# Retention and a gated MLP on one core: loads of two tokens to a partition, 64x64 quarters for every chunk, block 1 as Strassen

## The chip, the cores and the metric

The kernel runs on one core of a Trainium2 chip. A core has TensorE (matmuls into PSUM), VectorE, ScalarE, GpSimd and SyncE, each with its own queue of instructions that it works through in order; sixteen DMA engines serve the transfers that SyncE, ScalarE and GpSimd issue. The metric is the device time of one execution in microseconds. 304.59 us is the median of three runs of the kernel before (304.25 to 305.26).

## The reference

Eight batches of eight heads, 576 tokens and 64 columns go through a retention without softmax, and the 4608 resulting rows of 512 columns through an MLP with a cosine gate:

```python
scores = scale * np.matmul(q, k.transpose(0, 1, 3, 2))      # scale 1/8
Dmat = np.where(rel >= 0, gamma[:, None, None] ** rel[None, :, :], 0.0)
ret = scores * Dmat[None, :, :, :]
attn = np.matmul(ret, v)                                    # (8, 8, 576, 64)
x = attn.transpose(0, 2, 1, 3).reshape(4608, 512)
h = x @ w_in                                                # 512 x 2048
out = (h * np.cos(h)) @ w_out                               # 2048 x 512
```

All tensors are float32; the kernel multiplies in bf16.

## The kernel before

**Attention by chunks.** A batch is cut into four chunks of 128 tokens and one of 64 (`NCH` = 5). The decay is put into q and v: q is multiplied by gamma^position/8, v by gamma^-position (`decay`), k is only cast (`kcast`). For a chunk there are scores (k by q, both with the head's columns on partitions), a mask (`rt`, VectorE), the product with v, and a state: k transposed times v, summed over the chunks in the PSUM bank `st`, whose copy (`sb` in batches 0 and 1, `sn` later) gives the past's share to the next chunk. The result goes into `xt`, the MLP's input with columns on partitions (two ScalarE copies a chunk, split where the ring of `XR` = 1536 tokens wraps).

**Two ways to compute it.** Batches 2 to 7 use `quarters`: matmuls of 64x64, four of which use the four quarters of the array at once; `weave` interleaves two lists, one for each half of the rows, and a few products wait for an earlier one into the same bank. One call, a "visit", does past, own product and state of chunk r and the scores of chunk r+1 (of the next batch's chunk 0 after the last). Their k and q are turned by a DMA transpose (`turn_dma`). Batches 0 and 1 use `scores`, `rest`, `state_mm` and `state_copy`, with 128 tokens as the contraction. Their k and q come as quads (`quad`: four neighbouring tokens to a partition, two heads, all 512 tokens at once, runs of 1 KB), are cast by `quad_cast`, turned on TensorE against an identity (`quad_turn`: four matmuls and a copy), and k is turned back (`back`) for the state. Their last chunks are loaded as the later batches are: one token to a partition, runs of 256 B.

**MLP by blocks of 512 tokens.** Block j first computes h tile by tile (`mlp1`, 16 tiles `dt` of 128 columns: four matmuls of 512 tokens, a cosine on ScalarE into `cb`, a product on VectorE into `gt`), then the output. Blocks 0 and 1 do that plainly (`plain2`: four stripes of 128 tokens, each in four pieces of four matmuls, `out2` copies and stores). Blocks 2 to 8 use Strassen's seven products (`mlp2`) of half the size; sums of parts of `gt` (`ssum` into `ss`) and of w_out (`tsum` into `ts`, 16 of them, once) run on VectorE. The visits of batch j+1 stand between the products of block j; the casts and the DMA transposes of batch j+1 (`prep`) between the tiles of `mlp1`.

**The order.** Everything is written out by hand in `emit`; `Sched` adds the semaphores. Before the first tile of block 0 stand batch 0's quads, casts and turns, its chunks 0 to 2 and dummy matmuls (`idle`) that fill waits. Chunk 3 stands between the first tiles of block 0, which are cut into 256-token halves. Block 0's second product is 16 pieces, with batch 0's chunk 4, batch 1's turns, and its chunks 0 and 1 between them; block 1's first product is cut at 320 tokens, with batch 1's chunks 2 to 4; its second product, plain, has batch 2's five visits and the twelve remaining sums of w_out.

**Queues.** SyncE issues the loads in the order of `push`. GpSimd issues the weight loads, which cast to bf16: w_in slice 0 (`wi0`) once v of chunk 0 has landed, then the other three between casts, then four of w_out. A gate (`after`, "wi1") makes SyncE wait, ahead of the load of batch 0's chunk 4 and all of batch 1, until w_in slice 1 has landed. `pump` issues a load when its buffer among the 16 of `ld` is free in program order. ScalarE issues the stores.

The lines that the profile names: L264 loads, L287 and L293 weight loads, L299 copies and casts, L326 decay, L361/L409/L411 matmul groups, L433 and L704 masks, L502 and L504 cosine and gate, L526 and L544 Strassen sums, L660 `weave`.

Of the kernel before, what the change touches and what calls it, by code (L numbers as in the profile page):

```python
# [22 lines left out]
NR = 9  # L23
NL = 16
# [105 lines left out]
class _Kernel:  # L130
    def __init__(self, nc, es, q, k, v, w_in, w_out, out):
# [17 lines left out]
        self.QS = [sb(f"qs{i}", [128, 512], BF16) for i in range(4)]  # L149
        self.bQS = bufs(4)  # L150
        self.n_qs = 0
# [21 lines left out]
        self.SB = [sb(f"sb{i}", [128, NP * 128], BF16) for i in range(2)]  # L173
        self.bSB = [Buf() for _ in range(2)]
# [12 lines left out]
        self.IP = sb("ip", [128, NCH], F32)  # L187
        self.WV = sb("wv", [128, NCH * H_], F32)
        self.UQ = sb("uq", [128, NCH * H_], F32)
        self.IP4 = sb("ip4", [128, 4], F32)  # L190
        self.UQ4 = sb("uq4", [128, 4 * H_], F32)
        self.LG = sb("lg", [128, H_], F32)
        self.LP = sb("lp", [128, NCH * H_], F32)
        self.LP4 = sb("lp4", [128, 4 * H_], F32)
        self.bIP4, self.bUQ4, self.bLG, self.bLP, self.bLP4 = bufs(5)
        self.MK = sb("mk", [128, CH], BF16)
# [26 lines left out]
    def consts(self):  # L223
        s = self.s
        s.op("dve", lambda e: e.memset(self.IDLE.ap(), 0.0), writes=[self.bIDLE])
        s.op("pool", lambda e: e.iota(self.IP4.ap(), [[1, 4]], base=0, channel_multiplier=4,
                                      allow_small_or_imprecise_dtypes=True), writes=[self.bIP4])
        s.op("pool", lambda e: e.iota(self.IP.ap(), [[CH, NCH]], base=0, channel_multiplier=1,
                                      allow_small_or_imprecise_dtypes=True), writes=[self.bIP])
        s.op("dve", lambda e: e.memset(self.C_LN8.ap(), float(math.log(1.0 / 8.0))), writes=[Buf()])  # L230
        s.op("dve", lambda e: e.memset(self.C_PIH.ap(), float(math.pi / 2.0)), writes=[self.bC])
        for h in range(H_):
            t = s.op("dve", lambda e: e.memset(bass.AP(self.LG, h, [[H_, 128], [1, 1]]), self.lng[h]),
                     writes=[Buf()])
        self.bLG.w = [t]
        for t, b, fill, first, cmp in ((self.ID, self.bID, 1.0, 0.0, ALU.not_equal),
                                       (self.MK, self.bMK, 0.0, 1.0, ALU.is_ge)):
            s.op("dve", lambda e: e.memset(t.ap(), first), writes=[b])
            s.op("pool", lambda e: e.affine_select(t.ap(), t.ap(), pattern=[[1, CH]],
                                                   compare_op=cmp, fill=fill, base=0,  # L240
                                                   channel_multiplier=-1), reads=[b], writes=[b])
        for i in range(2):
            s.op("dve", lambda e: e.memset(self.SB[i].ap(), 0.0), writes=[self.bSB[i]])
        for lp, blp, ip, bip, n in ((self.LP4, self.bLP4, self.IP4, self.bIP4, 4),
                                    (self.LP, self.bLP, self.IP, self.bIP, NCH)):
            s.op("dve", lambda e: e.tensor_tensor(
                bass.AP(lp, 0, [[n * H_, 128], [H_, n], [1, H_]]), bass.AP(ip, 0, [[n, 128], [1, n], [0, H_]]),
                bass.AP(self.LG, 0, [[H_, 128], [0, n], [1, H_]]), ALU.mult), reads=[bip, self.bLG], writes=[blp])
        for t, b, sign, lp, blp in ((self.UQ4, self.bUQ4, 1.0, self.LP4, self.bLP4),
                                    (self.WV, self.bWV, -1.0, self.LP, self.bLP),  # L250
                                    (self.UQ, self.bUQ, 1.0, self.LP, self.bLP)):
            s.op("act", lambda e: e.activation(
                t.ap(), lp.ap(), AF.Exp, scale=sign, **(dict(bias=self.C_LN8.ap()) if sign > 0 else {})),
                reads=[blp, self.bC], writes=[b])
        s.op("act", lambda e: e.activation(self.JUNK.ap(), self.C_PIH.ap(), AF.Sin), reads=[self.bC])
# [3 lines left out]
    def fetch(self, key, src, dims, n):  # L259
        i = self.n_ld % NL  # L260
        self.n_ld += 1
        t = self.LD[i]
        dst = bass.AP(t, 0, [[DM, n]] + dims)
        t = self.s.dma("sp", f"ld{i}", lambda e: e.dma_start(dst, src), writes=[self.bLD[i]])  # L264
        self.got[key], self.busy[i] = i, True
        self.wtok[key] = t
# [5 lines left out]

    def load(self, b, r, xs="kqv"):
        ck = ck_of(r)
        for x in xs:
            src = bass.AP(self.src[x], (b * H_ * S_ + CH * r) * D_, [[D_, ck], [S_ * D_, H_], [1, D_]])
            self.fetch((x, b, r), src, [[D_, H_], [1, D_]], ck)

# [89 lines left out]
    def quad_turn(self, x, b, c, i, eng, bank=None):  # L368
# [10 lines left out]
        for u in (self.bKT if x == "k" else self.bQT)[s0:s0 + 4]:  # L379
            u.w.append(t)  # L380
# [669 lines left out]
```

## Time and profile before

| What | us |
|---|---|
| median of three runs | 304.59 (304.25 to 305.26) |
| the profiled execution | 302.51 |
| its span, first to last instruction | 300.6 |
| TensorE busy | 291.7 |
| VectorE busy | 222.7 |
| ScalarE busy | 169.8 |
| GpSimd busy | 107.0 |
| granted TensorE clock, mean | 0.999 |

A row of the table of stretches has the stretch (us from the span's start), its length, then for PE (matmuls), PEld (weight loads), DVE (VectorE), ACT (ScalarE) and POOL (GpSimd) the busy time and in brackets the instructions, then the granted clock, the share of the DMA engines (over 1 where packets overlap) and GB/s. A row of the chain, and of the timeline, has start, length, engine and what is done, written "out<-in"; in square brackets stands the idle time ahead of it and what ended it. A row of the groups has line, engine, operation, tiles, shapes and count, then busy time and mean ns of one, then the idle time ahead of the group. SPq and ACTq are the queues in which SyncE and ScalarE issue transfers.

### The profile page before, as it was taken

The numbers are of one execution on the slowest core, as the hardware profiler recorded it, in microseconds if no ns is written. First come the engines' busy times: TensorE is split into PE (matmuls) and PEld (weight loads), VectorE is DVE, ScalarE is ACT, GpSimd is POOL, SyncE is SP. The second block draws the span as 40 slices with busy tenths as digits, with TensorE's granted clock in tenths as the row PEclk, the third lists the DMA queues.
The fourth block names the chain that finished last, engine by engine and source line by source line (L and its number), as shares of the span: only waits on it lengthen the run. The fifth ranks groups of instructions, "written<-read, shape, count | busy, mean of one in ns | idle before, by whom it ended". The sixth has DMA issues, their size and how long they took to land.

```text
span 300.6 us, 7939 instructions
## 1 busy us (share of the span) xinstructions
PE 291.7 (97%) x3339; PEld 182.0 (61%) x3366; DVE 222.7 (74%) x422; ACT 169.8 (56%) x327; POOL 107.0 (36%) x127
## 2 busy tenths in 40 slices
PE   8899999999999999999999999999999999999995
PEld 3474455645454488548854776468646864684484
DVE  3666666767569997699669984998499749837963
ACT  6788535886247735673558355744575458416810
POOL 3670337656454653376445555454000000000000
PEclk9999999999999999999999999999999999999999
DMA  7999999999999998999999999999300130012013
GB/s 225 228 203 199 213 313 204 309 204 182 243 229 199 193 206 185 242 199 209 183 228 237 211 191 265 224 184 162 106 2 0 40 105 2 0 60 82 2 35 106
DMA packets 142419, 49.67 MB, mean 165 GB/s; under 512 B 126000, under 2 KB 141360, under 8 KB 142384
## 3 DMA queue, kind: packets, MB, share of 16 engines
q1 hardware_dynamic: 129376, 35.53, 66.5%
q10 hardware_dynamic: 8784, 9.44, 10.3%
q0 software_dynamic: 4224, 4.19, 8.6%
q8 instruction: 26, 0.43, 0.6%
q14 instruction: 9, 0.07, 0.1%
HBM read 36.70 MB, written 9.44 MB: 153 GB/s over the span
## 4 chain that ended last, share of the span: by engine, by line
PE 74%; DMA 12%; DVE 8%; SPq 2%; ACT 2%; issue 1%; POOL 0%; DVEq 0%; POOLq 0%
PE mm L409 53%; PE mm L411 11%; DMA ld<-in_q_dram 7%; DVE gt L504 4%; DVE ss L526 3%; DMA win<-in_moe_w_in_dram 3%; SPq L264 2%; PE sc L660 2%; DMA ld<-in_v_dram 2%; PE st L660 2%; PE mm L660 2%; PE sc L409 2%; PE po L660 2%; ACT cb L502 1%; DVE rt L704 1%
## 5 line engine op out<-in xcount | busy, mean ns | idle before, releaser
L502 ACT ACTIVATE cb<-mm,c_pih 128x512 bf16<-128x512 f32 (+3 forms) x156 | 100.8, 655 | 36.5 <-PE mm L411 36.2
L409 PE MATMUL mm<-xt,win 128*128 128x512 bf16 (+3 forms) x451 | 114.6, 363 | 1.3 <-DVE gt L504 0.3
L504 DVE TENSOR_TENSOR gt<-mm,cb 128x512 bf16<-128x512 f32 (+3 forms) x156 | 98.8, 645 | 20.0 <-ACT cb L502 17.1
L409 PEld LDWEIGHTS mm<-xt,win 128*128 128x128 bf16 x468 | 44.0, 98 | 48.3 <-DVE gt L504 4.0
L411 PE MATMUL mm<-xt,win 128*128 128x512 bf16 (+3 forms) x156 | 56.6, 363 | 0.4
L409 PE MATMUL mm<-wout,gt 128*128 128x256 bf16 (+1 forms) x298 | 49.6, 305 | 1.0 <-issue 0.6
L326 POOL TENSOR_TENSOR vb<-ld,wv 128x512 bf16<-128x512 f32 (+1 forms) x39 | 41.9, 1075 | 18.8 <-DMA ld<-in_v_dram 13.9
L704 DVE TENSOR_TENSOR rt<-sc,mk 128x512 bf16<-128x512 f32 (+1 forms) x60 | 35.3, 629 | 15.6 <-PE sc L660 13.4
L326 POOL TENSOR_TENSOR kq<-ld,uq 128x512 bf16<-128x512 f32 (+1 forms) x32 | 33.9, 1058 | 17.2 <-DMA ld<-in_q_dram 17.1
L299 POOL CAST kq<-ld 128x512 bf16<-128x512 f32 (+1 forms) x32 | 19.8, 620 | 51.9 <-DMA ld<-in_k_dram 46.7
L409 PE MATMUL mm<-ts,ss 128*128 128x256 bf16 x300 | 36.1, 273 | 0.0
L409 PEld LDWEIGHTS mm<-wout,gt 128*128 128x128 bf16 x306 | 27.7, 98 | 13.7 <-DVE gt L504 2.9
L409 PEld LDWEIGHTS mm<-ts,ss 128*128 128x128 bf16 x300 | 28.0, 98 | 4.7 <-issue 0.2
L299 ACT ACTIVATE u<-mm 128x512 f32<-128x512 f32 x21 | 12.5, 597 | 29.6 <-PE mm L411 29.6
L592 DVE TENSOR_TENSOR osb<-mm,u 128x512 f32<-128x512 f32 x21 | 14.3, 683 | 19.9 <-PE mm L411 16.1
L526 DVE TENSOR_TENSOR ss<-gt 128x512 bf16<-128x512 bf16 x56 | 28.1, 502 | 0.2
L411 PEld LDWEIGHTS mm<-xt,win 128*128 128x128 bf16 x156 | 15.3, 98 | 16.0
L299 ACT ACTIVATE sn<-st 128x256 bf16<-128x256 f32 x24 | 9.2, 383 | 27.6 <-PE mm L660 26.7
L299 ACT ACTIVATE xt<-po 128x256 bf16<-128x256 f32 (+2 forms) x39 | 15.1, 391 | 5.6 <-PE po L411 4.9
L411 PE MATMUL mm<-wout,gt 128*128 128x512 bf16 (+1 forms) x46 | 16.0, 347 | 0.1
L660 PE MATMUL po<-rt,vb 64*64 64x128 bf16 (+1 forms) x216 | 15.1, 218 | 0.3 <-DVE rt L704 0.3
L660 PE MATMUL mm<-rt,vb 64*64 64x128 bf16 (+1 forms) x216 | 15.1, 218 | 0.1
(144 smaller groups left out, 333.9 us busy)
## 6 DMA issues: line engine op xcount, KB each, us to landing
out_dram<-osb ACTq DMA_DIRECT2D x35, 256.0 KB, 3.7
ld<-in_k_dram SPq DMA_DIRECT2D x32, 256.0 KB, 4.7
ld<-in_q_dram SPq DMA_DIRECT2D x32, 256.0 KB, 5.0
ld<-in_v_dram SPq DMA_DIRECT2D x32, 256.0 KB, 5.8
win<-in_moe_w_in_dram POOLq DMA_DIRECT2D x4, 512.0 KB, 9.1
wout<-in_moe_w_out_dram POOLq DMA_DIRECT2D x4, 512.0 KB, 15.8
ld<-in_k_dram SPq DMA_DIRECT2D x8, 128.0 KB, 4.7
ld<-in_q_dram SPq DMA_DIRECT2D x8, 128.0 KB, 4.7
```

The lines of the kernel that those rows point to most:

```text
L264: t = self.s.dma("sp", f"ld{i}", lambda e: e.dma_start(dst, src), writes=[self.bLD[i]])
L299: fn = (lambda e: e.activation(o, x, AF.Copy)) if eng == "act" else (lambda e: e.tensor_copy(o, x))
L326: self.s.op(eng, lambda e: e.tensor_tensor(o, a, g, ALU.mult), reads=[bt, bw], writes=[bd])
L409: self.nc.tensor.matmul(o, a, b, **kw)
L411: return s.done("pe", self.nc.tensor.matmul(o, a, b, **kw), reads, writes)
L502: s.op("act", lambda e: e.activation(ci, mi, AF.Sin, bias=self.C_PIH.ap(), scale=1.0), reads=[bm, self.bC], writes=[self.bCB[i]])
L504: s.op("dve", lambda e: e.tensor_tensor(bass.AP(self.GT, dt * TB + o0, [[16 * TB, 128], [1, n]]), mi, ci, ALU.mult), reads=[bm, self.bCB[i ...
L526: self.s.op("dve", lambda e: e.tensor_tensor(self.s_(k, d), a, b, op), reads=rd, writes=[S[k - 1][p]])
L592: self.s.op("dve", lambda e: e.tensor_tensor(o, m, x, ALU.add), reads=[bm, self.bU[u]], writes=[self.bOSB[i]])
L660: inst = self.nc.tensor.matmul(o, a, c, **kw)
L704: self.s.op("dve", lambda e: e.tensor_tensor(bass.AP(self.RT[nr % 2][x], 0, p3), bass.AP(self.SC[x], 0, p3), bass.AP(self.MK, 0, [[CH, nk] ...
```

## The change

All loads now put two neighbouring tokens on a partition: partitions 0 to 63 hold heads 0 to 3, partitions 64 to 127 heads 4 to 7, in runs of 512 B (256 B for the 64-token chunk, one token to a partition there). A load is two DMAs, one for each half; for chunks 0 and 1 of batch 0 the second half is issued by ScalarE. With this layout every chunk of every batch goes through `quarters`, also in batches 0 and 1, and the 64-token chunk uses all 128 partitions. Quads, turning back, and the 128-token forms are gone. In batches 0 and 1 k and q are turned on TensorE chunk by chunk (`turn`, four matmuls and a ScalarE copy for each of the two), only chunk 4 of batch 1 by DMA. The order in a visit changes: past of one half into the other half's bank first, state and scores, then own. The output copies into `xt` read two token columns 64 apart and write them side by side.

The order of work changes at the start: chunk by chunk for batch 0; the first w_in load stands on GpSimd behind the casts of chunk 2, the second behind those of chunk 3, ahead of the rest. Block 0's first product is cut into 384 and 128 tokens for its first four tiles; the transpose of chunk (0,4) stands after the 12th tile and its scores after the 14th. Block 0's second product has all of batch 1's chunks 0 to 3 between its pieces, and all 16 sums of w_out. Block 1 goes into the same loop as blocks 2 to 8, so it is a Strassen block; the scores of batch 1's chunk 4 stand after its 14th tile.

```diff
+    def load(self, b, r, xs="kqv", engs=("sp", "sp")):
+        n = ck_of(r) // 64
+        for x in xs:
...
+            for h, e in enumerate(engs):
+                dst = bass.AP(self.LD[i], 64 * h * DM, [[DM, 64], [n * D_, 4], [1, n * D_]])
+                src = bass.AP(self.src[x], ((b * H_ + 4 * h) * S_ + CH * r) * D_, [[n * D_, 64], [S_ * D_, 4], [1, n * D_]])
+                t = self.s.dma(e, f"ld{i}", lambda e: e.dma_start(dst, src), writes=[] if h else [self.bLD[i]])
...
+            for x in range(2):
                 if r:
+                    past[x] = [(f"past{x}{y}", self.q_past(i, r, m, y, x), ck, [self.bQT[i], self.bSN[(r - 1) % 2]],
+                                [bXY[y]], None if y != x else f"past{1 - x}{x}") for y in (1 - x, x)]
+                own[x] = [(f"own{x}", self.q_own(i, r, m, x), ck, [self.bVB[i]] + self.bRT[r % 2], [bXY[x]], None)]
...
+            self.weave(past[0][:1] + state[0] + past[0][1:] + score[0] + own[0],
+                       past[1][:1] + score[1] + past[1][1:] + own[1] + state[1])
...
+        for b in range(B_):
             for r in range(NCH):
+                if (b, r) == (0, 4):
+                    self.push(self.after, "wi1")
+                self.push(self.load, b, r, "kqv", ("sp", "act") if b == 0 and r < 2 else ("sp", "sp"))
...
         self.idle(10)
+        casts(0, 0)
+        turns(0, 0, idle=2)
+        self.s.op("act", lambda e: e.activation(self.JUNK.ap(), self.C_PIH.ap(), AF.Sin), reads=[self.bC])
+        self.quarters(0, None, 0)
+        self.idle(2)
+        casts(0, 1)
         for r in range(1, 4):
+            turns(0, r, idle=2)
             if r < 3:
+                casts(0, r + 1)
+                self.w_in_load(r - 1)
+            self.quarters(0, r - 1, r)
+            self.idle(2)
+        for r in range(2, 4):
+            self.w_in_load(r)
         for r in range(4):
             self.w_out_load(r)
         self.pump()
+        banks = [None] * 2 + list(zip(self.SC, self.bSC))
+        for dt in range(4):
+            if dt == 2:
+                self.quarters(0, 3, None)
+            self.mlp1(0, dt, 0, 384, banks[dt])
+        for dt in range(4):
+            self.mlp1(0, dt, 384, 128, banks[dt])
+        self.order.append(3)
+        for dt in range(4, 16):
+            m1([dt], (0, 512))
+            if dt == 9:
+                self.casts(0, 4)
+                self.pump()
+            if dt == 11:
+                self.turn(0, 4, "kq", "act", (self.ST, self.bST))
+            if dt == 13:
+                self.quarters(0, None, 4)
...
+        sums(4)
+        self.cast("pool", "k", 1, 0)
+        piece("00 10 20 01 11 21")
+        sums(6)
+        self.cast("dve", "q", 1, 0)
+        self.cast("pool", "v", 1, 0)
         self.pump()
+        piece("02 12 22")
+        turns(1, 0, [(self.PO, self.bPO), (self.MM[3], self.bMM[3])])
+        casts(1, 1)
+        piece("03")
+        self.visit(1, 0)
+        self.out2(0, 0, "act")
+        piece("13")
+        turns(1, 1)
+        self.out2(0, 1, "act")
+        casts(1, 2)
+        self.visit(1, 1)
+        piece("23")
+        sums(1)
+        turns(1, 2)
+        self.out2(0, 2, "act")
+        casts(1, 3)
+        self.visit(1, 2)
+        piece("30")
+        sums(2)
+        turns(1, 3)
+        piece("31")
+        self.prep(1, 4)
+        self.visit(1, 3)
+        sums(3)
+        piece("32")
+        self.quarters(1, 3, None)
+        piece("33")
+        self.out2(0, 3, "act")
+        for j in range(1, NTB):
...
+                if j == 1 and dt == 13:
+                    self.quarters(1, None, 4)
```

A piece "13" is stripe 1, part 3 of the plain second product. In `casts` of batches 0 and 1 k and v go to GpSimd and q to VectorE; `prep` and chunk (0,4) give all three to GpSimd.

More of the change, by code (lines that the diff above doesn't have):

```diff
@@ L382, in back @@
[L382 to L389 removed]
+        blk, n = (0, 2 * n) if x == "kq" else (n if x == "q" else 0, n)
@@ L664, in quarters @@
     def quarters(self, b, r, n):
[L666 to L667 removed]
+        bXY, (nb, nr) = self.bXY, (n, 0) if r == NCH - 1 else (None, 0) if n is None else (b, n)
+        score, past, own, state = ([[], []] for _ in range(4))
         if nb is not None:
             nk, ni = ck_of(nr), slot(nb, nr)
[L670 removed]
+            nn = nk // 64
```

542 lines of the change are left out of this document (145 added, 397 removed).

## The prediction

> **What bounds the kernel now.** I read the page's first lines, then the table of stretches, then the chain that ended last, and last the queues in the first 60 us.
>
> ```profile
> span 300.6 us, 7939 instructions
> PE 291.7 (97%) x3339; PEld 182.0 (61%) x3366; DVE 222.7 (74%) x422; ACT 169.8 (56%) x327; POOL 107.0 (36%) x127
> ```
>
> ```profile
> 17.88:33.26 15.38, 15.20 (x106) 8.49 (x105) 10.46 (x19) 13.32 (x25) 3.37 (x5) 1.00 1.23 200
> 33.26:54.12 20.86, 20.37 (x195) 10.92 (x196) 13.49 (x24) 8.55 (x19) 11.93 (x15) 1.00 1.12 255
> 54.12:90.47 36.35, 35.18 (x454) 19.80 (x459) 24.17 (x49) 21.51 (x47) 20.05 (x23) 1.00 1.18 230
> 90.47:121.22 30.75, 30.52 (x415) 20.03 (x417) 26.15 (x47) 18.29 (x37) 15.34 (x17) 1.00 1.15 198
> 121.22:151.74 30.52, 30.42 (x414) 20.04 (x416) 24.85 (x45) 17.47 (x34) 16.33 (x17) 1.00 1.28 209
> 151.74:183.16 31.42, 30.80 (x415) 20.20 (x417) 26.26 (x45) 17.59 (x36) 16.26 (x18) 1.00 1.20 218
> 214.13:244.53 30.40, 30.30 (x414) 20.08 (x416) 23.54 (x45) 17.47 (x34) 0.00 (x0) 1.00 0.11 37
> ```
>
> The rows are: block 0's first product, its second product (with batch 1's attention in it), the whole plain block 1, then Strassen blocks 2, 3, 4 and 6. TensorE is busy 97% at full clock, so the time is its work plus its few waits: a change is worth what it takes off that row or makes it wait. A Strassen block costs 30.40 to 30.52 us undisturbed. VectorE with 24 to 26 of 30 us is the second limit; blocks 2 and 4 are 0.2 to 1.0 us longer for it. Ahead of block 0's first product lie 17.88 us of loading and attention.
>
> The first 50 us hang on transfers, as the chain shows:
>
> ```profile
> 4.89 6.11 DMA ld<-in_v_dram
> 12.23 8.81 DMA win<-in_moe_w_in_dram
> 21.82 11.62 DMA ld<-in_q_dram
> 33.58 1.04 POOL kq L326
> ```
>
> Batch 0's first v lands at 11.00 and releases the first w_in load. The second w_in slice lands at 21.04 and releases SyncE; behind that gate q of the 64-token chunk (0,4) lands only at 33.44, 12.4 us later, beside the remaining weight loads. GpSimd casts it at once, and TensorE here meets it late, inside the second product, so nobody waits.
>
> **Block 1 as Strassen: the gain.** Before, block 1 takes 36.35 us (first product in pieces, transposes back, batch 1's chunks 2 to 4, plain second product, batch 2's visits). After, it is like block 3, 30.45 us, plus the scores of chunk (1,4), 0.25 us (a visit of few matmuls, below): 30.7. Gain 5.65. Its 16 operand sums and three additions on VectorE are those of block 3's row, 24.85 us in 30.52, so they fit.
>
> **Loads and the gate: the first loss.** All of batch 0 now comes chunk by chunk in 512 B runs; the w_in loads stand on GpSimd behind the v casts, the first behind v of chunk 2 (9th load), the second behind v of chunk 3 (12th), before behind v of chunk 0.
>
> ```profile
> 5.00:10.00 5.00, 4.89 (x41) 2.85 (x40) 1.71 (x4) 3.42 (x6) 1.84 (x3) 1.00 1.10 317
> 10.00:15.00 5.00, 4.08 (x64) 2.35 (x63) 4.11 (x7) 3.50 (x7) 3.68 (x5) 1.00 1.24 187
> ```
>
> ```profile
> 3.63 0.61 POOL L299 CAST qs<-ld 128x512 bf16<-128x512 f32 x1 [1.48 <-DMA ld<-in_k_dram]
> 11.31 1.69 POOL L287 DMA_DIRECT2D win<-in_moe_w_in_dram  x2 [1.67 <-DMA ld<-in_v_dram]
> 12.99 1.07 POOL L326 TENSOR_TENSOR vb<-ld,wv 128x512 bf16<-128x512 f32 x1
> 33.58 1.03 POOL L326 TENSOR_TENSOR kq<-ld,uq 64x512 bf16<-64x512 f32 x1 [2.76 <-DMA ld<-in_q_dram]
> ```
>
> A 256 KB load took 0.83 us in 1 KB runs (317 GB/s) and 1.40 in a stretch with 256 B runs (187 GB/s); 512 B is unseen. I take 0.96, nearer the fast end since a weight load shares the slow stretch. The first load lands at 3.6, the 9th at 11.3, the 12th at 14.2; each v cast takes 1.07, so w_in 0 is issued at 12.4 (before 11.31) and w_in 1 at 15.3 (before 12.2). Two slices took 9.7 us from the first's issue to the second's landing; the second now starts 2 us later but finds no loads beside it, so the gate opens at about 21.8 (20.5 to 23.5 by the ends) against 21.04. Issuing two half loads costs SyncE about 0.5 us each; ScalarE takes half of chunks 0 and 1, which delays its tables by 3 us. That lies ahead of the next wait.
>
> The Trainium skill (DMA: Bandwidth & Descriptors, Specifications) says runs of 512 B and more move at line rate, smaller ones with read-modify-write. By it a load takes the 0.83 of the 1 KB runs and the time would come out 1.3 us lower; no trace here shows 512 B runs.
>
> Now the step that decides: the transpose of chunk (0,4) has moved from the second product into block 0's first product, after its 12th of 16 tiles. TensorE works in order and stands there until q is cast. The landing is gate + 12.4 = 34.2, since the load and its competitors are the same; the cast, 128x256 for 64x512, takes between half of 1.05 and 1.03, I take 0.55 (elements per partition set it): 34.8. When does TensorE get there? Chunk-wise attention of batch 0 is a ring of ScalarE copies (two transposed copies, state, two outputs per chunk) of about 3.4 us; I put the first product at 19.5 (17.88 to 21), and 12 tiles, one visit and small pieces take 11.7, so 31.2. It waits 3.6 us, and the prologue's own loss or gain vanishes in that wait. After it: transpose 0.2, four tiles and the scores 3.8: the second product starts at 38.8, not 33.26. Loss 5.5.
>
> **Block 0's second product: the second loss.** Before 20.86 us.
>
> ```profile
> 32.83 0.38 PE L409 MATMUL mm<-xt,win 128*128 128x512 bf16 x1
> 33.05 0.38 PE L411 MATMUL mm<-xt,win 128*128 128x512 bf16 x1
> 41.42 0.33 PE L409 MATMUL po<-ident,qs 128*128 128x128 bf16 x3
> 41.87 0.38 PE L409 MATMUL mm<-wout,gt 128*128 128x512 bf16 x1
> ```
>
> ```profile
> 229.59:230.12 0.53, 0.53 (x33) 0.49 (x33) 0.27 (x1) 0.43 (x1) 0.00 (x0) 1.00 0.00 0
> 231.97:232.74 0.77, 0.77 (x49) 0.68 (x49) 0.77 (x3) 0.00 (x0) 0.00 (x0) 1.00 0.00 0
> 234.59:235.43 0.84, 0.84 (x57) 0.75 (x57) 0.19 (x2) 0.00 (x0) 0.00 (x0) 1.00 0.07 20
> ```
>
> Matmuls of 512 columns start 0.216 us apart, so 16 pieces of four take 13.85; a chunk's eight transposes 0.45, four chunks 1.8; visits (1,0) to (1,3) and the closing one 0.53 + 0.77 + 3 x 0.84 = 3.8. Sum 19.5: the removed back-transposes and wider attention pay 1.4 us. But ScalarE stands between a transpose and its scores:
>
> ```profile
> L299 ACT ACTIVATE kqt<-mm 128x512 bf16<-128x512 f32 x8 | 4.6, 596 | 2.6 <-PE mm L411 2.4
> L299 ACT ACTIVATE xt<-po 128x256 bf16<-128x256 f32 x25 | 9.5, 379 | 4.8 <-PE po L411 4.8
> L299 ACT ACTIVATE xt<-po 128x128 bf16<-128x128 f32 x8 | 2.1, 274 | 0.0
> ```
>
> ```profile
> 49.81 0.60 ACT L299 ACTIVATE kq<-po 128x512 bf16<-128x512 f32 x1
> 50.30 0.59 ACT L299 ACTIVATE osb<-mm 128x512 f32<-128x512 f32 x1
> 51.34 0.60 ACT L299 ACTIVATE xt<-po 128x512 bf16<-128x512 f32 x1 [0.45 <-ACT osb L299]
> ```
>
> A copy is 0.60, 0.5 behind another; a store costs ScalarE 0.45 more, as it waits for its copy. After visit (1,0): two outputs 0.4, result copy 0.55 and store 0.45, k copy 0.6, q transpose 0.4 (its bank is the k transpose's, the only free one), q copy 0.6: 3.0 us, while TensorE has one piece and two transposes, 1.3. Wait 1.7. After visit (1,1): end of result copy and store 0.25, state and outputs 0.85, two copies 1.1: 2.2 against 1.3, wait 0.9. Visit (1,3) has one more piece between, 0.3; the last visit's masks and block 1's first tokens 0.2. So 19.5 + 3.1 = 22.6, a loss of 1.75. Copies that write pairs of tokens are unseen; the kqt copies that gather from four transposes cost the plain 0.6, so I take 0.38 (upper end 0.6, 2 us more here).
>
> Batch 1's loads: behind (0,4), k and q of (1,0) land by about 42, TensorE asks at 46.6; one chunk every 2.9 us follows, asked for every 3.5. Hidden; without that, each late load is paid in full. VectorE's ten weight sums ahead of q's cast (0.47 to 0.62 each) end at 45.5, also in time.
>
> **Later blocks.** Visits do the same columns. past of one half now waits for past of the other early in the visit, about 0.1 us each where state work fills in and more for the 64-token chunk; chunk 4 in four quarters gives 0.1 back. Range 0 to 0.25 a batch, I take 0.15, six batches 0.9. VectorE's masks of chunk 4 and GpSimd's casts of it halve, and block 2 no longer starts behind left-over weight sums: 0.35 plus 0.35 back (0 to 2, the excess of blocks 2 to 5). Net 0.2.
>
> **Sum.** 5.5 + 1.75 - 5.65 + 0.2 = +1.8 us. The profiled execution took 302.51 (span 300.6 and 1.9 around it), 2.1 below the median of 304.59; on it the sum gives 304.3, on the median **306.4**.
>
> **Rivals.**
> Faster, one way: ScalarE keeps up in the second product. Then it lasts TensorE's 19.5 and the time is 303.3. For it: 13.5 us of ScalarE work in some 15. Against: order, since two chunks' visits follow their transposes directly. It decides below 1.3 us of wait.
> Faster, another way: q of (0,4) is cast by 31, so no wait in the first product: 306.4 - 3.6 = 302.8. For it: faster loads, an earlier gate. Against: the 11.62 us of the chain's row, nothing in which is touched.
> Slower: TensorE comes out of the 3.6 us wait at half clock.
>
> ```profile
> 1.25 4.02 PE L409 MATMUL mm<-idle 128*128 128x512 bf16 x9 [1.25 <-DVE lg L233]
> 7.17 0.38 PE L411 MATMUL mm<-idle 128*128 128x512 bf16 x1
> ```
>
> At the start nine matmuls take 4 us where they later take 0.216 each: 4 us at half rate lose 2.0, time 308.4. The Trainium skill (TensorE: Matmul & The Clock Gate, Part 1) has the clock halved after one whole idle window of about 3.4 us that runs freely; by that rule a 3.6 us wait seldom holds a whole one. The trace of before has no such wait inside.
> Slower: the early waits inside visits cost 0.4 us and not 0.1, over 30 visits and more: 308.4.
>
> **How the numbers follow.** Forecast 0.48 (304.7 to 308.0), ScalarE keeps up 0.17, early q 0.08, half clock 0.12, slow visits 0.15. A difference under 0.3% (0.9 us, 303.7 to 305.5) cannot be told from none. Faster: most of the two fast rivals, 0.20. Same: the low end of the forecast and the rest, 0.15. Slower 0.65. The range: below, the fast rivals with little more, 302.5; above, half clock or slow visits with the upper gate, 309.4.
>
> **What would show it.** TensorE idle some 3.6 us near 31, in front of the transpose into st, released by GpSimd's kq cast behind the q load; the second product starting near 38.8; waits on ScalarE's kqt copies in front of sc in visits (1,1) and (1,2); block 1 starting near 61.4 and taking about 30.7. A first product without the wait, or a block 1 well above 31, makes the prediction wrong.

## The result, and the profile after

The changed kernel takes 317.44 us (316.86 to 317.5) against 304.42 for the kernel before (302.78 to 305.26), a ratio of 1.043 (95% interval 1.0385 to 1.0476). Slower was forecast, but at 306.4 us, and at most 309.4. The page of the profile after has in its first lines and its chain:

```profile
span 315.6 us, 8443 instructions
...
PE 292.9 (93%) x3548; PEld 184.8 (59%) x3574; DVE 224.0 (71%) x427; ACT 165.7 (53%) x318; POOL 101.7 (32%) x128
...
PE 71%; DMA 11%; SPq 10%; DVE 3%; ACT 2%; issue 2%; POOL 1%; DVEq 0%; POOLq 0%
PE mm L361 51%; PE mm L363 11%; SPq L269 8%; DMA ld<-in_q_dram 3%; DMA ld<-in_k_dram 3%; PE po L543 3%; PE sc L543 2%; PE mm L543 2%; SPq L328 2%; DMA win<-in_moe_w_in_dram 2%; DMA ld<-in_v_dram 1%; DVE ss L408 1%; PE st L543 1%; ACT kqt L294 1%; DMA kqt<-kq 1%
```

TensorE is busy about as long as before (292.9 us for 291.7), but that fills only 93% of the span. SPq takes 10% of the chain, for 2% before: SyncE's own issuing, of loads (L269) and of DMA transposes (L328). The stretches after: block 0's first and second product, block 1, block 2 and block 6.

```profile
20.41:42.47 22.06, 17.10 (x131) 8.31 (x134) 10.45 (x20) 12.51 (x23) 4.00 (x7) 0.92 1.22 206
42.47:66.58 24.11, 20.72 (x326) 11.36 (x328) 18.40 (x30) 10.86 (x28) 11.54 (x14) 1.00 0.88 218
66.58:103.74 37.16, 32.75 (x423) 21.26 (x426) 23.76 (x46) 18.12 (x35) 16.34 (x19) 0.95 0.84 175
103.74:134.78 31.04, 30.84 (x415) 20.29 (x417) 24.26 (x45) 17.57 (x34) 14.92 (x17) 1.00 0.94 202
229.27:260.19 30.92, 30.72 (x414) 20.34 (x416) 23.38 (x45) 17.57 (x34) 1.62 (x3) 1.00 0.26 65
```

| Stretch | before | after | difference | forecast |
|---|---|---|---|---|
| ahead of the first product | 17.88 | 20.41 | +2.5 | +1.6 |
| block 0, first product | 15.38 | 22.06 | +6.7 | +3.9 |
| block 0, second product | 20.86 | 24.11 | +3.2 | +1.75 |
| block 1 | 36.35 | 37.16 | +0.8 | -5.65 |
| from block 2 on | 210.1 | 211.9 | +1.7 | +0.2 |
| span | 300.6 | 315.6 | +15.0 | +1.8 |

Two stretches lost clock (0.92 and 0.95). In each TensorE first stood still; its longest waits:

```profile
PE sc L543 <- DMA kqt<-kq: 4.2, 2, 3.8
PE st L361 <- POOL kq L317: 4.1, 1, 4.1
```

The second is the wait that was forecast, in front of the transposes of chunk (0,4). The timeline of TensorE shows it and what follows:

```profile
32.42 0.38 PE L363 MATMUL mm<-xt,win 128*128 128x512 bf16 x1
36.91 0.34 PE L361 MATMUL st<-ident,kq 128*128 128x128 bf16 x3 [4.12 <-POOL kq L317]
37.09 0.22 PE L363 MATMUL st<-ident,kq 128*128 128x128 bf16 x1
37.14 0.84 PE L361 MATMUL mm<-xt,win 128*128 128x512 bf16 x3
37.79 0.62 PE L363 MATMUL mm<-xt,win 128*128 128x512 bf16 x1
38.21 1.48 PE L361 MATMUL mm<-xt,win 128*128 128x512 bf16 x3
```

From 37.14 to 40.05 the eight matmuls of two tiles take 2.91 us, not 1.73. The first wait stands in block 1: the visit that needs chunk (2,3) waits for its DMA transpose, and the product behind it runs at half clock, 3.19 us for 1.85. SyncE's queue in that time (x2 are the two halves of a load):

```profile
88.22 1.28 SPq L269 DMA_DIRECT2D ld<-in_v_dram  x2
89.55 1.34 SPq L328 DMA_TRANSPOSE kqt<-kq  x1
90.93 2.41 SPq L269 DMA_DIRECT2D ld<-in_k_dram  x2
93.38 1.28 SPq L269 DMA_DIRECT2D ld<-in_q_dram  x2
94.70 1.28 SPq L269 DMA_DIRECT2D ld<-in_v_dram  x2
96.02 1.29 SPq L328 DMA_TRANSPOSE kqt<-kq  x1
```

A load costs SyncE 1.3 us and more, a chunk 6.5, and the transposes of (2,3) at 89.55 and (2,4) at 96.02 stand in the queue behind loads for batch 3 that nobody needs yet. In the kernel before, each of these loads is one issue, and SyncE comes to the transpose of (2,4) at 79.99:

```profile
77.31 0.58 SPq L264 DMA_DIRECT2D ld<-in_k_dram  x1
77.93 0.71 SPq L264 DMA_DIRECT2D ld<-in_q_dram  x1
78.68 1.27 SPq L264 DMA_DIRECT2D ld<-in_v_dram  x1
79.99 3.46 SPq L338 DMA_TRANSPOSE kqt<-kq  x1
```

Between 60 and 95 us neither queue shows a pause between its rows, so that is no sign of a full one; a row also holds what SyncE waits for ahead of its issue. The sign is how little it waits. In that time SyncE waits 14.7 us in the kernel before, almost all of it in its transposes, for GpSimd's casts and for TensorE; in the changed kernel it waits 2.3 us. The largest entry of each:

```profile
SPq L338 <- POOL kq L299: 7.1, 4, 2.4
```

```profile
SPq L328 <- POOL kq L294: 1.3, 3, 0.8
```

So the theory to test: SyncE's second issue per load is the cause, through batch 2's transposes. The rival: TensorE's waits are separate losses, each paid where it stands.

### The profile page after: what moved, and what is told of

The parts are those of the page before. It is cut to its first block, busy times and chain, and to the rows that moved or that the text cites. A ratio compares the mean times of both kernels' runs of the same rounds, so it can differ in the third digit from the quotient of the medians.

```text
span 315.6 us, 8443 instructions
## 1 busy us (share of the span) xinstructions
PE 292.9 (93%) x3548; PEld 184.8 (59%) x3574; DVE 224.0 (71%) x427; ACT 165.7 (53%) x318; POOL 101.7 (32%) x128
## 4 chain that ended last, share of the span: by engine, by line
PE 71%; DMA 11%; SPq 10%; DVE 3%; ACT 2%; issue 2%; POOL 1%; DVEq 0%; POOLq 0%
PE mm L361 51%; PE mm L363 11%; SPq L269 8%; DMA ld<-in_q_dram 3%; DMA ld<-in_k_dram 3%; PE po L543 3%; PE sc L543 2%; PE mm L543 2%; SPq L328 2%; DMA win<-in_moe_w_in_dram 2%; DMA ld<-in_v_dram 1%; DVE ss L408 1%; PE st L543 1%; ACT kqt L294 1%; DMA kqt<-kq 1%
## 5 line engine op out<-in xcount | busy, mean ns | idle before, releaser
L384 ACT ACTIVATE cb<-mm,c_pih 128x512 bf16<-128x512 f32 (+2 forms) x144 | 98.0, 681 | 43.0 <-PE mm L363 42.8
L361 PE MATMUL mm<-xt,win 128*128 128x512 bf16 (+2 forms) x414 | 112.5, 379 | 1.5 <-ACT xt L294 0.6
L386 DVE TENSOR_TENSOR gt<-mm,cb 128x512 bf16<-128x512 f32 (+2 forms) x144 | 96.5, 678 | 24.2 <-ACT cb L384 21.0
L580 DVE TENSOR_TENSOR rt<-sc,mk 128x512 bf16<-128x512 f32 (+1 forms) x80 | 45.5, 605 | 26.6 <-PE mm L543 19.4
L363 PE MATMUL mm<-xt,win 128*128 128x512 bf16 (+2 forms) x144 | 54.7, 380 | 0.4
L361 PE MATMUL mm<-ts,ss 128*128 128x256 bf16 x345 | 42.7, 278 | 0.0
L361 PE MATMUL mm<-wout,gt 128*128 128x256 bf16 (+1 forms) x284 | 41.0, 290 | 0.7 <-issue 0.5
L543 PE MATMUL sc<-kqt 64*64 64x128 bf16 (+1 forms) x576 | 21.8, 217 | 7.5 <-DMA kqt<-kq 4.2
L363 PEld LDWEIGHTS mm<-xt,win 128*128 128x128 bf16 x144 | 14.2, 99 | 16.9 <-issue 0.6
L543 PE MATMUL st<-vb,kq 64*64 64x64 bf16 x512 | 21.8, 195 | 0.0
L543 PEld LDWEIGHTS sc<-kqt 64*64 64x64 bf16 x576 | 14.7, 107 | 10.4 <-DMA kqt<-kq 4.5
L543 PEld LDWEIGHTS st<-vb,kq 64*64 64x64 bf16 x512 | 15.3, 108 | 1.9 <-issue 1.7
```

What stands on the lines that cost most here:

```text
L361: self.nc.tensor.matmul(o, a, b, **kw)
L363: return s.done("pe", self.nc.tensor.matmul(o, a, b, **kw), reads, writes)
L384: s.op("act", lambda e: e.activation(ci, mi, AF.Sin, bias=self.C_PIH.ap(), scale=1.0), reads=[bm, self.bC], writes=[self.bCB[i]])
L386: s.op("dve", lambda e: e.tensor_tensor(bass.AP(self.GT, dt * TB + o0, [[16 * TB, 128], [1, n]]), mi, ci, ALU.mult), reads=[bm, self.bCB[i ...
L543: inst = self.nc.tensor.matmul(o, a, c, **kw)
L580: self.s.op("dve", lambda e: e.tensor_tensor(bass.AP(self.RT[nr % 2][x], 0, p3), bass.AP(self.SC[x], 0, p3), bass.AP(self.MK, 0, [[2 * CH, ...
```

## The experiments

The table has all runs: the ratio to the kernel before with its interval, when SyncE comes to the transpose of (2,4), and when block 2 starts (us, profiled execution). Each ratio is to the kernel before timed with the run. The runs were taken on several chips, so their ratios compare better than their medians.

| Run | ratio | (2,4) reached | block 2 |
|---|---|---|---|
| before | 1 | 79.99 | 90.47 |
| changed kernel | 1.0430 (1.0385 to 1.0476) | 96.02 | 103.74 |
| e1, one issue per load | 1.0166 (1.0104 to 1.0228) | 77.47 | 95.70 |
| e2, turns of (0,4) later | 1.0467 (1.0407 to 1.0527) | 95.11 | 104.71 |
| e3, two chunks ahead | 1.0319 (1.0255 to 1.0384) | 89.70 | 99.11 |
| e4, wait filled | 1.0388 (1.0341 to 1.0435) | 95.25 | 102.69 |
| e5, past behind the scores | 1.0386 (1.0350 to 1.0421) | 96.87 | 104.97 |
| e6, halves on GpSimd | 1.0832 (1.0758 to 1.0907) | 94.06 | 107.54 |
| e7, no gate | 1.0322 (1.0262 to 1.0382) | 93.12 | 100.52 |
| e8, turns a piece earlier | 1.0415 (1.0364 to 1.0465) | 95.82 | 103.86 |
| e10, gate behind (0,4) | 1.0348 (1.0288 to 1.0408) | 94.00 | 102.66 |
| e11, four repairs | 1.0152 (1.0107 to 1.0196) | 89.22 | 98.14 |
| e9, Strassen alone | 1.0294 (1.0249 to 1.0340) | 80.97 | 101.72 |
| e12, the same, VectorE's sums only | 1.0059 (1.0030 to 1.0088) | 80.71 | 91.45 |
| e14, the same, sums spread | 1.0085 (1.0058 to 1.0113) | 81.50 | 95.91 |
| e13, before, issues doubled | 1.0126 (1.0090 to 1.0162) | 86.40 | 91.96 |

**One issue per load (e1).**

```diff
-            for h, e in enumerate(engs):
-                dst = bass.AP(self.LD[i], 64 * h * DM, [[DM, 64], ...
+            e = engs[0]
+            dst = bass.AP(self.LD[i], 0, [[DM, 128], [n * D_, 4], [1, n * D_]])
...
```

> Each load is one DMA of 128 partitions, all issued by SyncE, instead of two of 64; as many bytes, in the same 512 B runs, but from heads 0 to 3 and twice the tokens, so heads 4 to 7 are left out of the result. Theory A (SyncE's queue: two issues of 0.62 to 0.66 us a load and 1.33 us a transpose are 5.3 us a chunk, with no pause from 27 us on; they make batch 0's loads, the weight gate and batch 2's DMA transposes late): block 1's wait of 4.0 us and its slow matmuls go (5.5 us), the gate opens about 1.5 us earlier and the first product's wait shrinks by as much: about 310 us. Theory B (the DMA engines are the limit: bytes and runs) and theory C (only the places of the transposes in the program count): within 1 us of the changed kernel, 317.

It took 308.33 us. A load is now 0.5 to 0.7 us of SyncE in these rows, and the queue runs ahead of the need (SyncE waits 9.9 us for casts between 60 and 95):

```profile
73.62 1.85 SPq L328 DMA_TRANSPOSE kqt<-kq  x1
75.52 0.65 SPq L269 DMA_DIRECT2D ld<-in_k_dram  x1
76.21 0.52 SPq L269 DMA_DIRECT2D ld<-in_q_dram  x1
76.77 0.66 SPq L269 DMA_DIRECT2D ld<-in_v_dram  x1
77.47 1.51 SPq L328 DMA_TRANSPOSE kqt<-kq  x1
```

With as many bytes, in the same runs, and the same instructions on TensorE, 8 of the 13 us are gone (5.0 us above the kernel before timed with it, where the changed kernel is 13.0 above): block 1 takes 32.44 us and waits for no transpose, and the wait in front of (0,4)'s transposes is 1.2 us. Most of the 5 us still lost lie in block 0's second product, here 25.65 us at a clock of 0.93, for 20.86 before.

```profile
37.61:63.26 25.65, 22.84 (x329) 12.34 (x327) 15.40 (x30) 10.85 (x28) 16.08 (x19) 0.93 1.18 281
63.26:95.70 32.44, 31.43 (x424) 20.63 (x425) 26.37 (x46) 18.13 (x35) 18.88 (x23) 1.00 1.20 226
```

**The wait of (0,4), removed or filled (e2, e4, e10).** e2 moves the transposes and scores of (0,4) into the second product; e4 puts 20 dummy matmuls in front of them; e10 loads (0,4) ahead of the gate.

```diff
 # e2
-            if dt == 11:
-                self.turn(0, 4, "kq", "act", (self.ST, self.bST))
-            if dt == 13:
-                self.quarters(0, None, 4)
...
-        piece("00 10 20 01 11 21")
+        piece("00 10 20 01")
+        self.turn(0, 4, "kq", "act", (self.ST, self.bST))
+        piece("11 21")
...
-        piece("02 12 22")
+        piece("02")
+        self.quarters(0, None, 4)
+        piece("12 22")
 # e4
             if dt == 11:
+                self.idle(20)
                 self.turn(0, 4, "kq", "act", (self.ST, self.bST))
 # e10
-                if (b, r) == (0, 4):
+                if (b, r) == (1, 0):
                     self.push(self.after, "wi1")
```

> The transpose of chunk (0,4) stands after the fourth piece of block 0's second product and its scores after the seventh, not inside the first product. Theory C (its place costs the 4.4 us wait and 2.1 us of half clock): 6 us less, 311. Theory A with a chain behind it: the second product starts 6 us earlier and then meets batch 1's loads, which land at the same times as now (k and q of (1,0) at 43.0 and 44.4, of (1,1) at 46.5 and 47.6), and block 1 meets the same late transpose, so most of it is given back: 315 to 317.

> Twenty dummy matmuls of 512 columns (4.3 us) ahead of the transpose of chunk (0,4), to fill TensorE's wait of 4.4 us there. If the clock after the wait is a cost of its own (tiles 12 to 15 took 5.6 us for 3.5): 2 us less, 315.4. If the clock does not follow the wait: 317.4, or more by what the dummies delay.

> The changed kernel with SyncE's gate one load later: chunk (0,4) is loaded ahead of the wait for w_in slice 1, only batch 1 and later stay behind it. Theory (SyncE's queue of issues sets when batch 2's transposes land and so when block 2 starts): six issues of about 0.6 us leave the backlog, block 2 starts 3.5 to 4 us earlier, near 100, and the time is 313 to 314. Rival 1 (the waits of TensorE are paid one by one): the 4.4 us wait and the 2.1 us of half clock behind it are gone and all of it stays, 310 to 311. Rival 2 (all is given back in block 1, as when the transposes of (0,4) were moved later): 317.

e2 took 318.21 us, above even the 315 to 317 expected. Its second product starts 6.4 us earlier (36.04 for 42.47) and block 2 starts 1 us later: all of it is given back in block 1, which takes 44.05 us at a clock of 0.88, with four waits for batch 2's transposes.

```profile
PE sc L543 <- DMA kqt<-kq: 8.6, 4, 3.5
```

e10 shows the same: 5.2 us earlier into the second product, only 1.1 into block 2, 6.7 us of waits for transposes in block 1. Its 314.34 us lie just above the 313 to 314 of its theory, and block 2 came later than the 100 expected; its profiled execution, 315.96 us, was slower than its median. e4 leaves the time that passes there as it was and changes only the clock behind it; the two stretches are of the changed kernel from the end of the wait on, and of e4 from its last dummies on:

```profile
37.14:40.05 2.91, 2.91 (x11) 0.88 (x8) 0.69 (x1) 1.28 (x2) 0.61 (x1) 0.61 1.21 211
```

```profile
37.00:40.40 3.40, 3.40 (x27) 1.58 (x26) 0.87 (x2) 1.97 (x3) 0.61 (x1) 1.00 1.20 214
```

The clock is 0.61 after an idle wait and 1.00 after one filled with matmuls. Block 2 starts 1.1 us earlier. The median, 315.32, is the one expected, 2.1 us below the changed kernel's; but measured against the kernel before timed with each, the gain is 1.0 us, and the intervals of the two ratios overlap. So the rival falls by e2 and e10: TensorE's wait in block 0 is not a loss by itself, as long as block 1 waits for SyncE.

**Fewer issues ahead of the transposes (e3, e7, e11).** e3 has two chunks loaded ahead instead of three (`AHEAD` 9 to 6). e7 removes the gate, so the queue starts earlier. e11 combines `AHEAD` 6 and e10's gate with e5 and e8 (below).

```diff
 # e3
-AHEAD = 9
+AHEAD = 6
 # e7
-                if (b, r) == (0, 4):
-                    self.push(self.after, "wi1")
```

> At most 6 load buffers in use ahead for batches 2 to 7 instead of 9, so that on SyncE the transpose of a chunk stands behind one chunk of loads less. Theory A: the transpose of chunk (2,3), issued at 89.55 and landed at 94.64, is issued about 5 us earlier; block 1's wait (4.0 us and 1.5 us of slow matmuls) goes and nothing else changes: 312. Theory B: no change, 317. If loads then land too late for their casts, the wait only moves: 317 or more.

> SyncE does not wait for the second w_in slice ahead of the load of chunk (0,4); the loads compete with the weights from 13 us on. Theory A: the gate held chunk (0,4) back; q of it lands near 25 instead of 36.2, the first product's wait of 4.4 us and its half clock (2.1 us) go, SyncE runs ahead by several us, and block 1's wait shrinks too: 309 to 311. Rival: the weights are then late and tiles or pieces wait for them: 317 or more.

> The changed kernel with four edits together: the gate behind chunk (0,4), two chunks of loads ahead instead of three, the second past of a visit behind the scores, and in block 0's second product every chunk's transposes a piece earlier. Theory: fewer issues ahead of batch 2's transposes take block 2's start from 103.7 to 96 or 97, the later blocks gain up to 0.5 us each; 307 to 310. Rival (each of the edits gains only where the others do not): 313, as with two chunks ahead alone. Neither theory expects it below the kernel before, since six half loads a chunk are still issued.

Each lets SyncE come to the transpose of (2,4) earlier, and block 2 follows 7.4 to 9.6 us behind it in every run of the changed kernel whose loads have both issues on SyncE; only in e1 the distance is 18.2 and something else decides. e3 took 313.15 us, 1 us above its theory, with 1.9 us of waiting for a transpose left. e7, 313.05 us, missed both its theory (309 to 311) and its rival (317 or more): its second product takes 26.53 us for 24.11, 1.5 of it TensorE's waits for w_out's loads, and block 1 still waits for transposes. e11, 308.6 us, is within its 307 to 310 and reaches e1's time and no more; its block 2 starts at 98.14, not at 96 or 97, and block 1 still takes 37.10 us.

**Second halves on GpSimd for batches 2 to 7 (e6).**

```diff
-                self.push(self.load, b, r, "kqv", ("sp", "act") if b == 0 and r < 2 else ("sp", "sp"))
+                self.push(self.load, b, r, "kqv", ("sp", "act") if b == 0 and r < 2 else ("sp", "pool") if b >= 2 else ("sp", "sp"))
...
```

The rest of the edit has the casts wait for both halves.

> From batch 2 on the second half of every load is issued by GpSimd and not by SyncE; data, bytes and runs as in the changed kernel. Theory A (SyncE's queue makes the transpose of chunk (2,3) late): three issues a chunk are gone from it, the wait of 4.0 us in block 1 and its slow matmuls go: 312. Theory B (DMA engines): 317. If GpSimd becomes the late one (15 issues of 0.8 us a batch beside 12.7 us of casts in 30 us): waits on casts instead, 317 or more.

330.63 us, far worse than theories A and B; of the three only the last, late casts and 317 or more, allows for it. The page's issues, of the changed kernel and of e6, show a part of why:

```profile
ld<-in_k_dram SPq DMA_DIRECT2D x62, 128.0 KB, 3.5
```

```profile
ld<-in_k_dram SPq DMA_DIRECT2D x38, 128.0 KB, 7.4
...
ld<-in_k_dram POOLq DMA_DIRECT2D x24, 128.0 KB, 7.2
```

An issue is no cheaper there (0.62 us, ahead of GpSimd's own casts), and from issue to landing takes twice as long, on SyncE's queue too. SyncE's transposes now wait for GpSimd's casts, 11.6 us between 60 and 95 us. Block 2 starts 3.8 us later than in the changed kernel, and 9.3 us more are lost behind that. Why SyncE's loads land later as well, and what the later blocks wait for, isn't settled.

**The order in visits and in the second product (e5, e8).** e5 puts the second `past` behind the scores in the first row of `weave`; e8 has the result copies and the transposes of each chunk a piece earlier (shown for chunk 1).

```diff
 # e5
-            self.weave(past[0][:1] + state[0] + past[0][1:] + score[0] + own[0],
+            self.weave(past[0][:1] + state[0] + score[0] + past[0][1:] + own[0],
 # e8
         piece("03")
-        self.visit(1, 0)
         self.out2(0, 0, "act")
         piece("13")
+        self.visit(1, 0)
+        self.out2(0, 1, "act")
         turns(1, 1)
-        self.out2(0, 1, "act")
         casts(1, 2)
-        self.visit(1, 1)
         piece("23")
         sums(1)
+        self.visit(1, 1)
```

> In a visit the past of the first half into its own bank, which waits for the past of the second half, stands behind the scores and no longer ahead of them; nothing else moves. In the changed kernel an undisturbed Strassen block takes 30.92 us (before 30.40), its visits 0.76, 0.70, 0.99, 0.99, 0.90 (before 0.53, 0.77, 0.84, 0.84, 0.84). Theory: the early wait is the whole of it: the visits fall to about 0.55, 0.70, 0.84, 0.84, 0.78, a block to 30.4, and the time by 3.5 us to 314. Rival: the longer visits come from the new access patterns: no change, 317.4.

> In block 0's second product the result copies stand a piece earlier and the transposes of chunks (1,1) and (1,2) ahead of a piece, so that ScalarE's copies run beside it. The second product takes 24.1 us, of which 19.5 are TensorE's work. Theory: ScalarE's chain is exposed, about 2 us come off the second product. At the end 2 us less only if block 1's late transpose does not give it back: with theory A it does, and the time stays at 316.5 to 317.5 while the second product shrinks to 22.

e5 makes an undisturbed block as short as before (30.40), where the changed kernel had 30.92:

```profile
230.16:260.54 30.38, 30.28 (x414) 20.17 (x416) 23.55 (x45) 17.56 (x34) 2.72 (x4) 1.00 0.30 80
```

So the wait for the other half's past is 0.5 us a block. 3.5 us in all were expected; the time from block 2 on falls by 0.9, and block 2 itself starts no earlier. The median is 316.13 for an expected 314. e8 misses: the second product stays at 24.4 us, for 22 expected. The waits for ScalarE's `kqt` copies shrink, and two for its result copies take their place:

```profile
PE mm L361 <- ACT osb L294: 2.1, 2, 1.2
PE sc L543 <- ACT kqt L294: 0.9, 2, 0.5
```

**Issues doubled in the kernel before (e13).** Each load of batches 2 to 7 as two transfers of four heads each, all else as before.

```diff
+                for h in range(2):
+                    dst = bass.AP(self.LD[i], 4 * h * D_, [[DM, ck], [D_, 4], [1, D_]])
+                    src = bass.AP(self.src[x], ((b * H_ + 4 * h) * S_ + CH * r) * D_, [[D_, ck], [S_ * D_, 4], [1, D_]])
+                    t = self.s.dma("sp", f"ld{i}", lambda e: e.dma_start(dst, src), writes=[] if h else [self.bLD[i]])
```

> The kernel before, with each load of batches 2 to 7 as two transfers of four heads each, the same bytes, places and 256 B runs; nothing else. Theory (SyncE's issues are the queue that decides): a chunk's six issues and its transpose then take 5.5 to 7 us of SyncE instead of about 5.1, batch 2's transposes land late, block 2 starts at 93 to 97 against 90.47, and the time is 307 to 311; most of the loss lies before block 2, since a block of 30.4 us has room for five chunks. Rival (the queue is bound by the bytes behind it, or the late start and the order of the changed kernel are needed for the loss): no difference, 303.5 to 305.

307.8 us, 1.3% slower, as the theory had it. Around the transpose of (2,4):

```profile
81.43 1.12 SPq L282 DMA_DIRECT2D ld<-in_k_dram  x2
82.60 1.88 SPq L282 DMA_DIRECT2D ld<-in_q_dram  x2
84.52 1.43 SPq L282 DMA_DIRECT2D ld<-in_v_dram  x2
86.40 1.20 SPq L349 DMA_TRANSPOSE kqt<-kq  x1
```

SyncE comes to it 6.4 us later than before, and visits begin to wait for transposes (0.8 us in block 1, none before). The place of the loss is not the one expected: its profiled execution, the fastest of its runs, spans 3.4 us more than that of the kernel before, and only 1.5 of these lie ahead of block 2, which starts at 91.96, not at 93 to 97.

**Block 1's Strassen form alone, on the old loads (e9, e12, e14).** The kernel before with `mlp2(1, ...)` in place of the sixteen pieces of `plain2`, and the sums that it needs put in three ways: four of the sums of w_out on GpSimd (e9), all on VectorE (e12), and fewer of them in block 1's first product (e14).

```diff
 # e12, behind block 1's tiles; the sums of gt (ssum) stand between these
-        self.order.remove(3)
-        for n in range(16):
-            self.plain2(1, n // 4, n % 4)
...
+        self.mlp2(1, [(2, r) for r in range(NCH)])
 # e9, ahead of it
+        while T:
+            self.tsum("pool", *T.pop(0))
 # e12 and e14, in mlp2 behind the fourth sums of gt
+        while self.T:
+            self.tsum("dve", *self.T.pop(0))
```

> The kernel before, with one part of the change alone: block 1's second product by Strassen's seven products, its loads, quads and plain attention of batches 0 and 1 as before. Block 1's tiles are reordered (the eight 192-token pieces stand after the 11th tile, so that the sums of gt come in time), five more sums of w_out stand on VectorE in block 0's second product, three in block 1's first, four on GpSimd. Theory: the Strassen form by itself is worth what the stretches say, the plain second product of 18.42 us against about 16.9 of a Strassen block: 1.5 us less, 302.9 (ratio 0.995), and the changed kernel loses that and more through its loads. Rival: VectorE's and GpSimd's added sums in front of block 1 push the tiles back by as much, then 304.4 or more.

> As the run before of block 1's Strassen form on the loads of the kernel before, but with none of the sums of w_out on GpSimd: seven more stand on VectorE in block 0's second product, three in block 1's first, two behind the sums for the last product. There GpSimd's four sums ran 1.14 us each in a row, and VectorE's bf16 sums, 0.42 us elsewhere, ended only with them, after 5.27 us; TensorE waited 4.4 us for the last tiles. Theory (those four sums were the loss): VectorE's sums are back at 0.4 to 1.3 us, the wait ahead of block 1's second product is gone, block 2 starts between 89 and 91 against 90.47, and the time is 302.9 to 304.1, about 1 us below the kernel before. Rival (the Strassen form itself is late there, since batch 2's casts and transposes land for a product that asks 1.5 us sooner): the wait turns up in batch 2's visits, released by a DMA transpose, and the time is above 306.

> Block 1's Strassen form on the loads of the kernel before, as in the run before of it without sums on GpSimd, but with VectorE's sums moved out of block 1's first product: nine of the sums of w_out in block 0's second product, three and half of the third sums of gt in block 1's second, and the 192-token pieces one by one behind the 512-token tiles. Theory (VectorE's queue took the gain): block 1's first product is back from 19.5 to about 18 us, the second stays near 16.8, block 2 starts near 89, and the time is 302.5 to 303.5. Rival (the sums only move the wait): block 0's second product or block 1's second gets longer by as much, and the time stays within 304 to 306.

All three lose, by 0.6 to 2.9%, where gains of up to 1.5 us were expected. e9 lost to a thing of its own, told below. Block 1's first and second product, before and in e12:

```profile
54.12:72.05 17.93, 17.49 (x159) 10.50 (x159) 13.26 (x27) 15.53 (x33) 10.03 (x11) 1.00 1.15 225
72.05:90.47 18.42, 17.69 (x296) 9.30 (x301) 10.91 (x23) 5.98 (x15) 10.03 (x12) 1.00 1.20 235
```

```profile
55.21:74.73 19.52, 17.94 (x159) 10.37 (x157) 17.65 (x36) 15.44 (x32) 11.16 (x12) 1.00 1.07 232
74.73:91.45 16.72, 16.72 (x350) 14.14 (x349) 13.83 (x29) 7.12 (x19) 9.62 (x11) 1.00 0.99 193
```

The second is 1.7 us shorter than the 18.42 of before, as expected, and the first 1.6 us longer than its 17.93: VectorE has 17.65 us of work there where it had 13.26, and over the whole execution TensorE waits 2.1 us for its `gt`, 0.3 before. The profiled execution of e12, 302.89 us, is the fastest of its twelve; the median, 305.84, lies between its theory and its rival, and where the 1.7 us by which it exceeds the kernel before are lost isn't shown. e14 spreads the sums, and both products get longer (20.79 and 18.82); its 306.52 us are above its theory and just above its rival. So in these three placings VectorE's sums cost what the Strassen form gains; e14's theory, that they only stood in the wrong place, falls. No version beat the kernel before.

## Why the prediction was wrong, point by point

- **SyncE's issues: the step that failed.** "Issuing two half loads costs SyncE about 0.5 us each … That lies ahead of the next wait" had the price a little low (0.62 us, 0.66 apart) and the cover wrong. I never added the queue up: six issues and a transpose are 5.3 us of a chunk at best and 6.5 where it mattered, from the gate at 23 us on, in the queue that also has batch 2's transposes. It was not a delay that the next wait covers but a backlog that grew up to block 1. Halving the issues takes back 8 of the 13 us (e1), taking issues out of the way of the transposes takes back 3 (e3), and doubling them in the kernel before costs 4 (e13).
- **Loads at 0.96 us each.** For chunks 2 and 3, SyncE alone issues a half every 0.66 us, so a load every 1.32; v of chunk 3 landed at 16.48, not 14.2. w_in 1 went out at 17.54 for 15.3, and the gate opened at 23.18, in the range of 20.5 to 23.5 given.
- **The wait in front of (0,4).** Place, releaser and size were right (4.1 us against 3.6; q landed 13.0 us behind the gate against 12.4). Of the 3.7 us by which the second product started later than forecast, 2.1 are the later gate, landing and cast, and 1.6 the half clock.
- **Half clock, a rival given 0.12.** It happened, twice, after waits of 4.1 and 3.8 us. The Trainium skill (TensorE: Matmul & The Clock Gate, Part 1) has the clock halved after one idle window of about 3.4 us; the trace agrees for these two waits. I had read the rule as speaking against it; the wait came out longer than the window. Other runs differ from the rule, and their measurement decides: the same wait was 2.95 us in e3 and 2.91 in e5, shorter than the window, and the clock behind it was 0.62 and 0.64 over the next 4.5 and 4.7 us.
- **Second product, 22.6.** It took 24.1 us. The waits for ScalarE's copies came in the two visits named, and TensorE's idle time is near the forecast (3.4 us for 3.1); the term that was too small is TensorE's own work, 20.72 us at full clock for 19.5. e8 shows that the waits move rather than vanish, as they would if ScalarE's ring of copies were the limit.
- **Block 1, 30.7.** The largest single miss, 6.5 us: 4.2 of waits for transposes and 1.3 of half clock behind the longest. TensorE's work was a little low: it is 31.43 us at full clock in e1, for 30.42 in block 3 and 0.25 added. Without those waits the block takes 32.44 us there. The comparison with block 3 took the transposes as given, since block 3 has them early.
- **Later blocks, +0.2.** +1.7 us. The visits cost 0.5 us a block where I took 0.15 a batch; e5 shows the cause that was named. Over blocks 2 to 6 that is 2.6 us. Of the excess of blocks 2 to 5 only 0.2 came back, since block 4 took 32.61 us with 1.2 of waits for VectorE's masks (30.92 in e1); 0.7 came back behind block 6. The rival of slow visits was added up wrongly: 0.3 us more over 30 visits are 9 us, not the 2 of its 308.4.
- **Rivals on the fast side** did not occur; ScalarE does not keep up, and q of (0,4) is late. That the time came out slower, as forecast, is no merit of the sum: the first losses were forecast at their places and too small, and the gain in block 1 that was to pay for them never came.

## What to carry to other kernels

When a load is split in two, add up the issuing queue over a whole stretch, with everything else that stands in it, as one would an engine: here six issues of 0.65 us and a transpose filled it, though the same bytes went through faster with half the issues (e1). Look for the last thing in that queue that somebody waits for; a wait removed ahead of it bought nothing in e2, and in e10 1.1 us of the 5.2 by which the second product started earlier. Also price a faster form of a product with the sums that it needs on another engine (e12).

## What the runs showed of the hardware

VectorE's bf16 sums take as little as 0.42 us. In e9 GpSimd ran six operations in a row, and a sum of VectorE's beside them took 5.27 us; it ended 0.3 us after the fifth of them. The last tiles stood behind it, and TensorE waited 4.4 us for them. VectorE first, then GpSimd:

```profile
74.80 5.27 DVE L526 TENSOR_TENSOR ss<-gt 128x512 bf16<-128x512 bf16 x1
```

```profile
74.16 1.31 POOL L326 TENSOR_TENSOR kq<-ld,uq 64x512 bf16<-64x512 f32 x1
75.43 1.03 POOL L326 TENSOR_TENSOR vb<-ld,wv 64x512 bf16<-64x512 f32 x1
76.43 4.65 POOL L544 TENSOR_TENSOR ts<-wout,ts 128x512 bf16<-128x512 bf16 x4
```

The Trainium skill (SBUF — State Buffer, Who interferes with whom) says that a VectorE operation with two SBUF inputs and a GpSimd operation that reads SBUF lock each other out for a whole instruction. The trace fits this and goes further: the sum got no turn between the first five of GpSimd's instructions.

The clock also dropped without a long wait. In e1 a piece of the second product ran at 0.50 behind visits whose waits were 0.8 us and less, one after the other; the changed kernel had nearly the same waits there at 1.00. What tips it is open.

```profile
50.50:52.40 1.90, 1.27 (x49) 1.19 (x48) 0.47 (x1) 1.08 (x2) 1.31 (x3) 0.73 1.12 313
52.40:54.20 1.80, 1.80 (x12) 0.64 (x6) 1.80 (x4) 0.94 (x3) 1.73 (x4) 0.50 1.17 322
```
